# Two chunks of 256 tokens, q's tiles by halves, wider exponentials of the transposed q and reciprocal products on GpSimd, in a linear attention with a maxout feed-forward

## The chip, the core and the metric

The kernel runs on one core of one Trainium2 chip. TensorE (PE) multiplies into PSUM, eight banks of 128 x 512 floats. VectorE (DVE), ScalarE (ACT) and GpSimd (POOL) do the elementwise work; SyncE (SP) issues most DMAs. The metric is the device time of one execution, as a median of several runs, in microseconds (us).

## What is computed

Batch 8, 8 heads, 576 tokens, head size 64, 128 features; then a feed-forward of 512 to 768 to 512 on the 4608 tokens.

```python
def phi(x):
    proj = np.einsum('bhsd,df->bhsf', x, w_phi)
    proj = proj - np.max(np.abs(proj), axis=-1, keepdims=True)
    return np.concatenate([np.exp(proj), np.exp(-proj)], axis=-1)
q_p, k_p = (phi(q), phi(k))
kv = np.einsum('bhsf,bhsd->bhfd', k_p, v)
z = np.sum(k_p, axis=2)
num = np.einsum('bhsf,bhfd->bhsd', q_p, kv)
den = np.einsum('bhsf,bhf->bhs', q_p, z)[..., None] + 1e-06
x = (num / den), heads side by side: 4608 x 512
h = np.maximum(np.maximum(x @ w1, x @ w2), x @ w3)
out = h @ w_out
```

## The kernel before, in words

The attention is cut into 16 units, each four heads of one batch row. A unit has 18 tiles of 128 tokens for q and for k. 16 of q's tiles are the first 512 tokens of the four heads, the last two the ends (64 tokens a head). For each unit:

- q and k are loaded and cast to bf16 (units 0 to 3 by a casting DMA from GpSimd's queue; later units by a DMA from SP's queue and copies on GpSimd, L509, tile qk_bf). They are transposed into qkT, by TensorE for units 0 to 3 (tps, L494) and by a DMA later (L513).
- Projections psq and psk (L535), with tokens on the partitions. VectorE takes the row maxima mq and mk (L547). ScalarE writes the exponentials Ek of k, with both signs (L544), and em from mk (L557). GpSimd multiplies v by em into vab (L565). TensorE sums kvps (L586), copied to kv_sb (L592).
- Transposed projections psm of q, with features on the partitions (L606), in matmuls of 512 columns, one PSUM bank each. ScalarE takes the exponentials Eq of both signs from each bank (L612, eight instructions of 512 columns and two of 256 a unit).
- The tiles sq = exp(-2 mq) on ScalarE (L618, L619). The products psn of Eq and kv_sb (L637), for one head at a time: five tiles of 65 columns (64 values and the denominator) in one bank for each sign. VectorE scales the first bank by sq into y (L640, node kind "xu"), adds the second (L643, "xw"), takes the reciprocal of the denominators (L645, "xr"); the product with it goes to x_sb, on GpSimd or VectorE (L647, "x").
- x_sb is transposed into xT, by TensorE and a copy for units 0 to 5 (pxT, L657, L660), by a DMA on SP's queue later (L664).

The feed-forward subtracts w1 from w2 and w3 first (L762), so that the maximum is a ReLU and a max, and adds x @ (w1 @ w_out) again at the end. It works on nine chunks of 512 tokens: chunk b is the first 512 tokens of batch row b, chunk 8 the ends of all rows. A chunk is 12 up products of four 128 x 512 matmuls each (ups, L687). The first six are evacuated as a ReLU ("t1", on ScalarE L695 or VectorE L697), the other six as a maximum on VectorE ("h", L693), into hT. Then each of its four token tiles takes four matmuls from xT (L715) and six from hT (L720) into ops, a copy to osb (L728) and a store (L735).

The order of the work is written out in the string PLAN: each word names a node, the engine that does it, the buffer slots it takes, and after the @ the due time that a planner gave it. The kernel issues the nodes in the order of the words, so each engine has a fixed order and waits at its head. The due times and the costs in the nodes only sort the words; nothing waits for a clock. Before, a node of a unit for the product is one of these:

```python
n_ = nd("xu", {"DVE": 0.42}, lambda ...: nc.vector.tensor_tensor(...), ...)
n_ = nd("x", {"POOL": 1.42, "DVE": 0.74}, None, [n_], [y, rden, x_sb])
```

The keys are the engines allowed; PLAN says which one is taken.

Of the kernel before, what the change touches and what calls it, by code (L numbers as in the profile page):

```python
# [25 lines left out]
HU = 4  # L26
# [10 lines left out]
EARLY = 2  # L37
WARM = 28.0
# [46 lines left out]
8S0@0.7 5G0@1.2 6S@1.3 2S@1.9 0G@2.1 4G@2.6 10S0@3.1 92G1@3.5 9A@3.9 93G@4.3 11S0@4.4 177G2@5.2 7D@5.4 3D@5.9 176G@6.0  # L85
15T0@6.0 13T1@6.7 16D0@6.7 1173G@6.8 14D@7.4 34T000200@7.5 29T34@7.7 36A@8.0 38D@8.0 24T51@8.1 19T67@8.4 31A@8.4
94D@8.6 27D@8.7 20A@8.9 28D@9.3 26A@9.4 12G@9.8 32D@9.9 35A@9.9 96G@10.0 17T5@10.2 21A@10.4 178S0@10.4 18D@10.5
252G0@10.5 33D@10.8 30A@10.9 58T0500@10.9 23D@11.4 25A@11.4 253G@11.4 63T34@11.5 95S@11.7 60A@11.9 22D@12.0 39T16@12.1
1176G@12.2 401S0@12.3 62A@12.3 37D@12.6 44A0@12.8 59A@13.0 97T7@13.1 42D@13.2 47G0@13.2 45G@13.5 61A@13.5 43D@13.5
101T2@13.6 99T0@13.7 98D1@13.9 65A@14.0 100D@14.5 48A@14.5 108T117511@14.6 66A@14.7 46G@14.8 112D@15.1 41A@15.2  # L90
118T01@15.3 64A@15.5 102D@15.7 68T7@15.9 111D@15.9 67A@15.9 152T211@16.1 69A@16.4 122D@16.5 103T34@16.6 40A@16.7
256G@16.8 70A@17.0 51G@17.0 107D@17.1 110A@17.3 181G@17.3 113T60@17.3 49G@17.5 400S0@17.7 153A@17.7 106D@17.8
123T73@17.9 154A@18.2 117D@18.4 109A@18.5 184T2@18.6 50G@18.8 119A@18.9 116D@19.0 52T065@19.2 71A0@19.4 185D0@19.6
104A@19.6 115A@20.1 1174G@20.2 53D@20.2 182T2@20.3 126D@20.4 54A@20.6 121D@20.8 128A0@20.8 55T65@21.0 105A@21.0
127D@21.4 130G0@21.5 132A@21.5 183D@21.7 124A@21.7 75T47@21.8 57A@22.0 114A@22.2 56D@22.3 72T52@22.5 76D0@22.5
135A@22.7 134G@22.8 125A@22.8 186T6@22.9 73D@23.0 147T04@23.1 120A@23.1 187D@23.5 149A@23.6 80T35@23.6 77D@23.7
83T16@23.9 150A@24.1 133G@24.1 254D1@24.1 74D@24.2 1185T7@24.3 148A@24.6 81D1@24.6 1183T2@24.9 84D@25.0 151A@25.0
129G@25.4 82D@25.5 1187T3@25.5 1186A0@25.5 85D@25.9 142T51@26.2 78D0@26.3 139T040@26.4 131A@26.5 179D@26.5 1188D@26.6
1184A@26.6 79G0@26.7 180S@26.8 136T76@27.0 328S@27.4 146A@27.6 140D@27.8 259T2@27.9 86D1@28.0 327S@28.0 137A@28.1
138D@28.2 155A0@28.3 87G@28.4 261T4@28.4 141D@28.4 145A@28.5 159T36@28.6 329S@28.6 260D1@28.6 88T7@28.9 144A@29.0  # L100
262D@29.3 228T100@29.3 206T112011@29.4 160D0@29.5 143A@29.6 1175G@29.8 255S@29.9 210D@29.9 164T43@30.1 230A@30.1
161D@30.2 89A@30.4 156T52@30.4 165D1@30.7 90T6@30.8 157D@31.1 167T74@31.2 91A@31.4 166D@31.5 257T5@31.7 168D@31.9
207A@32.0 223T36@32.2 208A@32.4 169D@32.5 1193T7@32.6 225A@32.7 258D@32.9 224A@33.3 1D4@33.5 170D1@33.7 1189T5@33.9
158D@34.0 1194A@34.2 209D@34.4 227A@34.7 171D0@34.7 229A@35.2 197T7023@35.3 162D0@35.5 1190A@35.5 303T111@35.8
174T4@36.0 200D@36.0 304A@36.1 1191T5@36.3 226A@36.4 163D@36.6 202A@36.9 1177G@37.3 175D@37.4 305A@37.4 172T6@37.6
1192A@37.8 205D@37.9 1195T1@37.9 173A@38.3 204D@38.5 198A@39.0 201D@39.1 188T2654@39.3 1179G@39.4 203A@39.4
1201T7@39.8 199A@39.9 196D@40.0 1196A@40.4 192D@40.6 1199T0@40.7 193A@40.9 191D@41.2 1202A0@41.4 1178G@41.5
272T00152300@41.7 1200D@41.8 1209T7@42.2 278A@42.4 195D@42.4 189A@42.9 280D@43.0 1207T0@43.1 277A@43.4 407G2@43.6
276D@43.7 194A@43.8 1205T2@44.0 279D@44.3 1208A@44.3 403G@44.5 211A0@44.8 1203T4@44.8 1181D@44.9 190A@45.0 404G@45.1
1210D@45.5 274A@45.5 406G@45.7 281T63@45.8 218T01@45.9 1206A@46.0 284D@46.2 1217T7@46.2 1204A@46.5 285D@46.5  # L110
212G0@46.5 1180D@46.8 219A@47.0 1215T6@47.1 1182D@47.4 283A@47.5 221A@47.8 1211T4@48.0 1216D@48.2 282A@48.2 273A@48.5
1218D@48.8 1221T3@48.8 222A@49.0 213G@49.0 1212D@49.5 214A@49.5 220A@49.6 1213T2@49.7 275D@50.1 231A0@50.1 1219T4@50.6
1214D@50.8 1222D@51.5 405G@51.5 263T5176@51.5 331G0@51.8 408S0@51.9 215T002@52.0 1220D@52.1 264A@52.3 334G@52.3
267D@52.7 265A@52.9 333G@53.0 293T34@53.2 270D@53.3 217A@53.5 1223T5@53.5 332G@53.6 216A@53.8 266D@53.9 297A@54.1
240T20@54.4 271D@54.5 286A0@54.7 1224T@54.7 474S0@54.8 294A@54.9 287G0@55.0 241D0@55.1 296A@55.4 335S2@55.4 242D@55.7
295A@55.8 243T71@56.0 1225A0@56.3 232T02@56.4 298T34@56.8 268A@56.9 233D1@56.9 1231T5@57.1 244D@57.4 289A@57.4
288G@57.5 299A@57.6 245D@57.9 235T70@58.0 300A@58.2 1232T@58.3 544S@58.3 234D@58.3 269A@58.7 246D0@58.8 543S0@58.9
236D@59.0 302A@59.2 237D@59.6 475S@59.6 409T01612311@59.7 1233A1@59.9 247G0@60.0 238D1@60.1 290T007@60.2 413D@60.4
410A@60.5 473S@60.8 414A@60.9 417D@61.0 239G@61.4 306A0@61.4 1227T6@61.4 292D@61.6 291A@61.6 301A@62.0 416D@62.0
315T70@62.3 412D@62.6 310T24@62.6 415A@62.7 1228T@63.0 316D1@63.2 411A@63.3 311D0@63.6 317D@64.0 318T13@64.3 312D@64.4  # L120
1229A2@64.5 366T0200@64.7 549G0@64.8 319D@64.9 371T75@64.9 369A@65.2 307T46@65.3 479G2@65.4 320D@65.4 250T1@65.6
374A@65.7 308D@65.9 480G@66.0 1235T3@66.0 373A@66.1 321D1@66.3 251D@66.5 367A@66.6 322G1@66.7 1236T@66.9 309D@67.0
372A@67.1 313D0@67.6 370A@67.6 314D@67.9 550G@68.1 375A@68.1 325T7@68.2 248T2@68.5 368A@68.6 326D@68.8 323T6@68.8
614S0@68.9 249A@69.1 439T0111@69.3 478G@69.3 324D@69.4 427T75@69.5 684S@69.5 442A@69.7 354T104200@69.9 1237D3@69.9
547G@70.0 1241T6@70.1 330S1@70.1 441A@70.2 477G@70.5 431D@70.5 443A@70.7 357D@70.9 1247T3@70.9 440A@71.2 358D@71.2
1242D0@71.5 429A@71.7 336T4701@71.9 356A@71.9 430D@72.2 1248A@72.2 1249T6@72.5 344D@72.6 428A@72.7 620G1@72.8
355A@73.0 343D@73.2 1259T5@73.3 546G@73.5 1250A@73.6 340D@73.8 548G@74.1 341A@74.1 345T6023@74.3 619G@74.3 339D@74.4
613S0@74.5 342A@74.7 1243T4@74.8 349D@75.0 615S@75.1 346A@75.2 352D@75.7 338A@75.7 1245T1@75.7 1244A@76.2 348D@76.3
402S@76.3 1261T6@76.6 353D@76.9 1230S@76.9 359A0@77.0 337A@77.2 361G0@77.4 1255T4@77.5 1260D@77.5 481S1@77.5 362A@77.7
351A@77.9 1262D@78.1 1257T5@78.3 1246A@78.3 1256D@78.7 379A0@78.8 347A@79.0 418T2167@79.3 1258D@79.4 350A@79.5  # L130
# [161 lines left out]
def kernel(  # L292
# [562 lines left out]
```

## Time and profile before

| | before |
|---|---|
| median of 3 runs | 292.28 us (291.39 to 293.37) |
| the profiled execution's own time | 291.29 us |
| its span, first to last instruction | 289.5 us |
| PE busy | 268.4 us, 93% |
| DVE busy | 236.1 us, 82% |
| ACT busy | 199.7 us, 69% |
| POOL busy | 157.1 us, 54% |
| granted TensorE clock | 0.99 |

A group of the profile is a line: source line, engine, operation, tiles out<-in, shapes and count, then busy us and mean ns of one, then the idle time ahead of it and what ended it. Neighbours on an engine overlap, so a mean is longer than the distance from one start to the next. PE's busy time counts matmuls that wait in the pipeline, so a busy PE is not a PE at its peak. In the chain of work that ended last, PE has 76%, ACT 5%, DVE 4%, and the up products (L687) alone 30%.

### The profile page before, as it was taken

The page shows a single profiled execution, that of the slowest core. Times are in us where ns is not written, and L with a number is a line of the kernel's source. Part 1 is how long each engine was busy: PE and PEld are TensorE (multiplying, and loading weights), DVE is VectorE, ACT ScalarE, POOL GpSimd, SP SyncE. Part 2 cuts the span into 40 slices and gives each one's busy share as a digit, 9 for nine tenths or more (in the row PEclk, how much of TensorE's full clock was granted, in tenths as well). Part 3 has the DMA queues.
Part 4 walks back from the last instruction along what each step waited for, and adds up shares of the span by engine and source line. Part 5 has one row for each costly group of instructions (what it writes and reads, how often), then busy time and mean ns, then how long its engine had stood idle before and what let it go on. Part 6 is the DMA issues. An engine that isn't in the chain of part 4 may idle for free.

```text
span 289.5 us, 8537 instructions
## 1 busy us (share of the span) xinstructions
PE 268.4 (93%) x3461; PEld 151.7 (52%) x3502; DVE 236.1 (82%) x466; ACT 199.7 (69%) x486; POOL 157.1 (54%) x162
## 2 busy tenths in 40 slices
PE   1878899799999899999999999999999999999993
PEld 1557654356547555664565455655455564444442
DVE  1898889989997989999999988989999985246421
ACT  2797899598997698699855798999968470200020
POOL 8359478765757737672488593881935752000000
PEclk9997999999999999999999999999999999999998
DMA  8999992496699989957999898799045023020036
GB/s 156 227 247 255 253 271 87 77 207 209 210 258 223 262 238 340 240 138 163 334 211 175 221 267 202 233 102 224 20 121 151 5 48 84 0 109 2 36 148 143
DMA packets 70663, 49.93 MB, mean 172 GB/s; under 512 B 47072, under 2 KB 58720, under 8 KB 70624
## 3 DMA queue, kind: packets, MB, share of 16 engines
q1 hardware_dynamic: 65232, 44.25, 60.9%
q0 software_dynamic: 5312, 5.08, 10.8%
q8 instruction: 27, 0.44, 0.6%
q10 hardware_dynamic: 80, 0.07, 0.1%
q14 instruction: 12, 0.10, 0.1%
HBM read 34.67 MB, written 9.44 MB: 152 GB/s over the span
## 4 chain that ended last, share of the span: by engine, by line
PE 76%; ACT 5%; DVE 4%; issue 3%; DMA 2%; POOL 1%; SPq 0%; ACTq 0%; DVEq 0%
PE ups L687 30%; PE ops L720 13%; PE ops L715 9%; PE psn L637 7%; PE kvps L586 5%; PE psq L535 4%; ACT Eq L612 4%; PE psm L606 3%; PE pm L788 2%; DMA xT<-x_sb 2%; DVE hT L693 1%; PE psk L535 1%; ACT Ek L544 1%; DVE mk L547 1%; DMA out_dram<-osb 1%
## 5 line engine op out<-in xcount | busy, mean ns | idle before, releaser
L687 PE MATMUL ups<-xT,w_bf 128*128 128x512 bf16 x413 | 98.3, 379 | 2.7 <-DVE w_bf L762 1.5
L544 ACT ACTIVATE Ek<-psk 128x512 bf16<-128x512 f32 (+1 forms) x160 | 83.7, 581 | 15.9 <-PE psk L535 11.1
L565 POOL TENSOR_TENSOR vab<-v_raw,em 128x1152 bf16<-128x1152 f32 (+1 forms) x36 | 68.6, 1927 | 37.2 <-ACT em L557 33.4
L612 ACT ACTIVATE Eq<-psm 128x512 bf16<-128x512 f32 (+1 forms) x160 | 81.2, 585 | 7.8 <-PE psm L606 7.4
L687 PEld LDWEIGHTS <-w_bf 128*128 128x128 bf16 x432 | 39.8, 98 | 49.2 <-DVE w_bf L762 2.4
L720 PE MATMUL ops<-wout_bf,hT 128*128 128x512 bf16 (+1 forms) x217 | 50.7, 373 | 0.3 <-issue 0.2
L547 DVE TENSOR_REDUCE mq<-psq 128x4 f32<-128x512 f32 (+1 forms) x80 | 48.9, 627 | 1.4 <-PE psk L535 1.1
L547 DVE TENSOR_REDUCE mk<-psk 128x4 f32<-128x512 f32 (+1 forms) x80 | 48.2, 627 | 2.1 <-PE psk L535 0.9
L647 POOL TENSOR_TENSOR x_sb<-y,rden 128x640 bf16<-128x640 f32 x22 | 28.1, 1285 | 21.4 <-DVE rden L645 19.4
L693 DVE TENSOR_TENSOR hT<-hT,ups 128x512 bf16<-128x512 bf16 x54 | 35.8, 681 | 4.5 <-PE ups L687 3.9
L728 ACT COPY osb<-ops 128x512 f32<-128x512 f32 (+1 forms) x22 | 12.8, 581 | 37.6 <-PE ops L720 33.9
L640 DVE TENSOR_TENSOR y<-psn,sq 128x325 f32<-128x325 f32 x64 | 29.9, 489 | 4.2 <-PE psn L637 3.3
L637 PEld LDWEIGHTS <-Eq 128*128 128x128 bf16 x640 | 26.0, 99 | 11.9 <-issue 3.4
L720 PEld LDWEIGHTS <-hT 128*128 128x128 bf16 x222 | 20.4, 98 | 21.5 <-issue 0.3
L643 DVE TENSOR_TENSOR y<-y,psn 128x325 f32<-128x325 f32 x64 | 29.5, 484 | 1.3
L637 PE MATMUL psn<-kv_sb,Eq 128*128 128x65 bf16 x640 | 28.3, 196 | 1.7 <-DVE y L640 0.8
L695 ACT ACTIVATE hT<-ups 128x512 bf16<-128x512 f32 x31 | 18.3, 620 | 14.2 <-PE ups L687 13.9
L697 DVE TENSOR_SCALAR hT<-ups 128x512 bf16<-128x512 f32 x23 | 15.7, 686 | 14.1 <-PE ups L687 14.0
L535 PE MATMUL psq<-wph,qkT 64*128 64x128 bf16 x288 | 25.8, 225 | 0.7 <-ACT Ek L544 0.3
L535 PEld LDWEIGHTS <-qkT 64*128 64x128 bf16 x576 | 18.7, 97 | 14.7 <-issue 12.5
L535 PE MATMUL psk<-wph,qkT 64*128 64x128 bf16 x288 | 25.4, 225 | 0.3 <-DVE mq L547 0.2
L715 PE MATMUL ops<-xT 128*128 128x512 bf16 x82 | 23.8, 380 | 1.2 <-DVE mk L547 0.3
(59 smaller groups left out, 270.9 us busy)
## 6 DMA issues: line engine op xcount, KB each, us to landing
v_raw<-in_v_dram SPq DMA_DIRECT2D x16, 576.0 KB, 6.5
out_dram<-osb SPq DMA_DIRECT2D x32, 256.0 KB, 2.9
k_raw<-in_k_dram SPq DMA_DIRECT2D x12, 576.0 KB, 5.4
q_raw<-in_q_dram SPq DMA_DIRECT2D x12, 512.0 KB, 6.0
w_bf<-in_moe_w_dram POOLq DMA_DIRECT2D x3, 768.0 KB, 14.5
q_raw<-in_q_dram SPq DMA_DIRECT2D x16, 64.0 KB, 5.1
qk_bf<-in_k_dram POOLq DMA_DIRECT2D x3, 288.0 KB, 9.4
qk_bf<-in_q_dram POOLq DMA_DIRECT2D x3, 256.0 KB, 10.6
```

What stands on the lines that cost most here:

```text
L535: nc.tensor.matmul(ps()[:, i, :], lhsT=cols[r0:r0 + D, :], rhs=wph[r0:r0 + D, :], start=True, stop=True)
L544: "ek", {"ACT": 0.485 if n == 4 else 0.28}, lambda s=s, t0=t0, n=n, psk=psk: nc.scalar.activation(Ek[s]()[:, t0:t0 + n, :], psk()[:, 0:n, ...
L547: reds.append(nd(kind, {"DVE": 0.607 if n == 4 else 0.34}, lambda ps=ps, m=m, t0=t0, n=n: nc.vector.tensor_reduce(m()[:, t0:t0 + n], ps()[ ...
L565: made.append(any_of(n_, lambda n_, g=g, t0=t0, t1=t1: (nc.vector if n_.eng == "DVE" else nc.gpsimd).tensor_tensor(vab()[:, g, t0:t1, 0:D] ...
L612: "eq", {"ACT": 0.485 if n == 4 else 0.28}, lambda s=s, t0=t0, n=n, psm=psm: nc.scalar.activation(Eq[s]()[:, t0 * P:(t0 + n) * P], psm()[: ...
L637: nc.tensor.matmul(psn[g]()[:, c, :], lhsT=Eq[g]()[:, t0:t0 + P], rhs=kv()[:, pr, ab, g, :], start=True, stop=True)
L640: n_ = nd("xu", {"DVE": 0.42}, lambda pr=pr, ab=ab, psn=psn, y=y: nc.vector.tensor_tensor(y()[:, ab], psn[0](), sq()[:, 2 * pr + ab, :].un ...
L643: sums.append(nd("xw", {"DVE": 0.42}, lambda ab=ab, psn=psn, y=y: nc.vector.tensor_tensor(y()[:, ab], y()[:, ab], psn[1](), ALU.add), [n_] ...
L687: nc.tensor.matmul(ups(), lhsT=w_bf[i + 1][:, ct, j * P:(j + 1) * P], rhs=tokens_of(ct), start=(ct == 0), stop=(ct == CT - 1))
L693: nc.vector.tensor_tensor(hT()[:, j, :], hT()[:, j, :], ups(), ALU.max)
L715: nc.tensor.matmul(ops_()[:, 0:width], lhsT=tile_of(ct, tt), rhs=line_w[c_i > MOVE][:, ct, cols], start=(ct == 0), stop=False)
L720: nc.tensor.matmul(ops_()[:, 0:width], lhsT=hT()[:, j, tt * P:(tt + 1) * P], rhs=wout_bf[:, j, cols], start=False, stop=(j == JT - 1))
```

## The change

Five edits and a new PLAN, with the costs of many nodes set anew:

- Tiles of q are reordered: of each pair of heads, first the two tiles of tokens 0 to 255 of both, then those of 256 to 511 (tile_of_q; the casts on GpSimd become two of four tiles each). The products psn, y, the reciprocals and x go by halves (two tiles a head, then two and the end), two heads at a time.
- All eight banks are one tile (banks). psm takes two neighbouring banks, and one ScalarE instruction takes the exponential of 1024 columns.
- The scaling xu may go to ScalarE, which does it with one instruction of 65 columns for each tile and head, scaled by a column of sq. In the new PLAN 37 of 64 do.
- The product with the reciprocal is on GpSimd in all 64 cases. Units 14 and 15 are transposed by TensorE too (SOON; there reciprocals are taken for each pair of heads).
- Chunks 0 and 7 are done as two of 256 tokens, chunk 8 as 384 and 128; a chunk's first half waits for the first halves of its units only.

```diff
+SOON = (0, 1, 14, 15)
+SPLIT = (0, 7)
...
+    def tile_of_q(t):
+        pr, half, ab, c = t // 8, t // 4 % 2, t // 2 % 2, t % 2
+        return 8 * pr + 4 * ab + 2 * half + c if t < MT else t
...
+                    for half in range(2):
+                        copy_on[n_.eng](
+                            qk()[:, t0 + 4 * half:t0 + 4 * half + 4, col:col + D].rearrange("p (a j) d -> p a j d", a=2),
+                            raw_part(u, c, t0, t0 + 8).rearrange("p (a h j) d -> p a h j d", a=2, h=2)[:, :, half])
...
-                        "eq", {"ACT": 0.485 if n == 4 else 0.28}, lambda s=s, t0=t0, n=n, psm=psm: nc.scalar.activation(
-                            Eq[s]()[:, t0 * P:(t0 + n) * P], psm()[:, 0:n * P], EXP, scale=1.0 - 2.0 * s), [a], [psm, Eq[s]], locks=[psm]))
+                psm = Buf(slots.setdefault("bank", Slots(8)), lambda b: banks[:, b.index:b.index + 2, :], 2)
...
+                n_ = nd("eq", {"ACT": 0.905 if len(parts) == 2 else 0.265}, lambda s=s, psm=psm, to=to: nc.scalar.activation(
+                    to(), psm(), EXP, scale=1.0 - 2.0 * s), [a], [psm, Eq[s]], locks=[psm])
...
-                n_ = nd("xu", {"DVE": 0.42}, lambda pr=pr, ab=ab, psn=psn, y=y: nc.vector.tensor_tensor(
-                    y()[:, ab], psn[0](), sq()[:, 2 * pr + ab, :].unsqueeze(2).to_broadcast([P, 5, W]), ALU.mult),
+                n_ = nd("xu", {"DVE": 0.07 + 0.14 * nt, "ACT": 0.2 * nt}, None, [a, n_sq], [psn[0], sq, y], locks=[psn[0]])
...
+                    for ab in range(2):
+                        for c in range(nt):
+                            nc.scalar.mul(y()[:, pr, ab, c, :], psn[0]()[:, ab, c, :], sq()[:, pr, half, ab, c:c + 1])
...
-            n_ = nd("x", {"POOL": 1.42, "DVE": 0.74}, None, [n_], [y, rden, x_sb])
+                    m = nd("x", {"POOL": 0.155 + 0.209 * nt}, None, [n_], [y, rden, x_sb])
...
-        if u < X_PE:
+            if u < X_PE or u in SOON:
...
+        for c0, n in ([(0, 256), (256, 256)] if b in SPLIT else [(0, SM)]):
...
+    for b0, b1 in ((0, 6), (6, 8)):
+        chunk(B, lasts[b0:b1], b0 * ST, (b1 - b0) * ST, lambda ct, b0=b0, b1=b1: xT[:, b0:b1, ct, SM:SM + ST],
```

In PLAN's new order the four weight loads stand together on GpSimd's queue ahead of unit 0's vab; the first 384 tokens of chunk 8 stand between units 12 and 14; four subtractions of the weights are on GpSimd and two on VectorE (before three and three).

More of the change, by code (lines that the diff above doesn't have):

```diff
@@ L90 @@
[L90 to L94, printed above, removed]
@@ L273, in fill @@
             if b.pool is pool and b is not spare:
-                x = spans.setdefault(id(b), [b.index, n.start, n.end])
-                x[1], x[2] = min(x[1], n.start), max(x[2], n.end)
+                for i in range(b.width):
+                    x = spans.setdefault((id(b), i), [b.index + i, n.start, n.end])
+                    x[1], x[2] = min(x[1], n.start), max(x[2], n.end)
     for n in order:
@@ L336, in fixed, with make @@
         return Buf(pool, lambda b: tiles[b.index])
+    banks = psum.tile([P, 8, SM], FP32, name="banks")
     def bank(name, shape, dtype=FP32):
-        pool = slots.setdefault("bank", Slots(8))
-        return Buf(pool, lambda b: psum.tile(shape, dtype, name=name, tag=f"b{b.index}"))
+        per = 1
+        for n in shape[1:]:
+            per *= n
+        names = "abcd"[:len(shape) - 1]
+        sizes = {c: n for c, n in zip(names, shape[1:])}
+        def make(b):
+            x = banks[:, b.index, :]
+            x = (x if dtype == FP32 else x.bitcast(dtype))[:, 0:per]
+            return x.rearrange(f"p ({' '.join(names)}) -> p {' '.join(names)}", **sizes) if len(names) > 1 else x
+        return Buf(slots.setdefault("bank", Slots(8)), make)
     nodes = []
@@ L650, in attention @@
[L650 to L662 removed]
+        divs, done = [], []
@@ L663, in xdma @@
+        if not done:
             def xdma():
@@ L728, in ev @@
                     copy_on[n_.eng](part()[:, 0:width], ops_()[:, 0:width])
-                e = ff("osb", {"ACT": 0.61, "DVE": 0.62} if halves == 1 else {("ACT", "DVE")[i]: 0.35}, None, [a], [ops_, part],
+                e = ff("osb", {"ACT": 0.53, "DVE": 0.61} if halves == 1 else {("ACT", "DVE")[i]: 0.35}, None, [a], [ops_, part],
                        locks=[ops_])
@@ L798 @@
         rows = out[b * S:b * S + SM, :].rearrange("(p j) n -> p j n", j=SM // P)
-        chunk(b, units[2 * b]["done"] + units[2 * b + 1]["done"], lambda ct, b=b: xT[:, b, ct, 0:SM],
-              lambda ct, tt, b=b: xT[:, b, ct, tt * P:(tt + 1) * P],
-              lambda tt, rows=rows: [(rows[:, tt, :], slice(0, P))], 1)
+        hT = buf("hT", 2, [P, JT, SM], BF16)
+        for c0, n in ([(0, 256), (256, 256)] if b in SPLIT else [(0, SM)]):
+            ready = [x for u in (2 * b, 2 * b + 1) for half in range(2) if 256 * half < c0 + n and c0 < 256 * half + 256
+                     for x in units[u]["done"][half]]
+            chunk(b, ready, c0, n, lambda ct, b=b, c0=c0, n=n: xT[:, b, ct, c0:c0 + n],
+                  lambda ct, tt, b=b: xT[:, b, ct, tt * P:(tt + 1) * P],
+                  lambda tt, rows=rows: [(rows[:, tt, :], slice(0, P))], 1, hT)
         if b == MOVE:
-            for n in units[UNITS - 2]["done"] + units[UNITS - 1]["done"]:
-                n.deps += straights[0] + lines[1]
+            for u in (UNITS - 2, UNITS - 1):
+                for n in units[u]["done"][0] + units[u]["done"][1]:
+                    n.deps += straights[0] + lines[1]
     lasts = []
@@ L821, in fn @@
         def fn():
-            idler = psum.tile([P, SM], FP32, name="idler", tag=f"b{i}")
-            nc.tensor.matmul(idler, lhsT=idle, rhs=idle.unsqueeze(1).to_broadcast([P, 4, P]), start=True, stop=True)
+            nc.tensor.matmul(banks[:, i, :], lhsT=idle, rhs=idle.unsqueeze(1).to_broadcast([P, 4, P]), start=True, stop=True)
         return fn
```

497 lines of the change are left out of this document (269 added, 228 removed).

## The prediction

> **What bounds the kernel now.** I read the busy time of each engine first, cut into stages, then the waits, then the groups by shape, then single lines of the timeline. The stages are cut at the first up product (tile ups, L687) of chunks 0 to 7. The columns of the windows are the engines' busy time with the count of instructions, the granted clock, the DMA share and GB/s.
>
> ```profile
> core 0: us, PE busy (x) PEld busy (x) DVE busy (x) ACT busy (x) POOL busy (x), PEclk, DMA share, GB/s
> 0.00:43.10 43.10, 32.29 (x557) 22.69 (x558) 32.84 (x73) 32.71 (x80) 27.82 (x37) 0.96 1.11 234
> 43.10:74.80 31.70, 29.73 (x401) 16.51 (x404) 30.01 (x55) 26.34 (x63) 23.75 (x23) 1.00 0.57 136
> 74.80:105.80 31.00, 30.08 (x414) 16.95 (x420) 27.74 (x57) 26.19 (x66) 19.90 (x21) 1.00 0.99 249
> 105.80:135.40 29.60, 29.04 (x406) 16.14 (x413) 28.77 (x58) 25.24 (x66) 16.87 (x16) 1.00 0.87 229
> 135.40:163.20 27.80, 27.04 (x396) 15.47 (x401) 26.66 (x54) 19.28 (x48) 19.70 (x20) 1.00 1.01 224
> 163.20:196.30 33.10, 32.16 (x508) 18.55 (x512) 30.18 (x63) 31.19 (x78) 22.87 (x21) 1.00 0.91 211
> 196.30:223.50 27.20, 26.99 (x372) 14.73 (x372) 25.75 (x50) 23.55 (x56) 14.76 (x13) 1.00 0.52 122
> 223.50:246.70 23.20, 22.88 (x244) 12.47 (x245) 18.15 (x38) 9.69 (x25) 11.46 (x14) 1.00 0.23 57
> 246.70:289.50 42.80, 38.20 (x184) 18.22 (x186) 15.96 (x25) 5.48 (x10) 0.00 (x0) 0.97 0.24 74
> ```
>
> To be seen: in six stages from 43 to 223 us VectorE is busy 89 to 97% of the time beside a TensorE that is rarely idle, ScalarE 69 to 94%, GpSimd 54 to 75%. From 247 us on TensorE works alone. So an edit pays if it takes work off VectorE, as long as nothing else fills in its place.
>
> ```profile
> POOL x_sb L647 <- DVE rden L645: 19.4, 9, 4.8
> POOL qk_bf L486 <- DMA q_raw<-in_q_dram: 6.1, 2, 3.6
> 249.31 11.82 PE ups L687 x54
> 70.11 4.03 ACT Eq L612 x8
> ```
>
> The first two lines are waits (total, times, longest), the others pieces of the chain (start, us, what). GpSimd waits for rows of VectorE and, once, 3.6 us for the ends of q at the start. TensorE alone does a 512-column matmul in 11.82/54 = 0.219 us, and ScalarE an exponential of 512 columns in 4.03/8 = 0.50.
>
> ```profile
> L544 ACT ACTIVATE Ek<-psk 128x512 bf16<-128x512 f32 x128 | 73.3, 623 | 13.2 <-PE psk L535 10.7 <-DVE mk L547 2.4
> L544 ACT ACTIVATE Ek<-psk 128x256 bf16<-128x256 f32 x32 | 12.6, 412 | 2.7 <-DVE mk L547 2.3 <-PE psk L535 0.4
> L565 POOL TENSOR_TENSOR vab<-v_raw,em 128x1152 bf16<-128x1152 f32 x28 | 59.5, 2146 | 37.2 <-ACT em L557 33.4 <-PE psn L637 3.0 <-DMA v_raw<-in_v_dram 0.8
> L565 POOL TENSOR_TENSOR vab<-v_raw,em 128x576 bf16<-128x576 f32 x8 | 9.0, 1160 | 0.0
> L647 POOL TENSOR_TENSOR x_sb<-y,rden 128x640 bf16<-128x640 f32 x22 | 28.1, 1285 | 21.4 <-DVE rden L645 19.4 <-PE psn L637 1.2 <-DVE v_raw L478 0.6
> L647 DVE TENSOR_TENSOR x_sb<-y,rden 128x640 bf16<-128x640 f32 x10 | 10.5, 1051 | 0.2
> L640 DVE TENSOR_TENSOR y<-psn,sq 128x325 f32<-128x325 f32 x64 | 29.9, 489 | 4.2 <-PE psn L637 3.3 <-ACT kv_sb L592 0.7
> L619 ACT ACTIVATE sq<-mq 128x4 f32<-128x4 f32 x16 | 3.7, 234 | 0.0
> 20.44 0.29 ACT L618 ACTIVATE sq<-mq 128x16 f32<-128x16 f32 x1
> 20.55 0.27 ACT L619 ACTIVATE sq<-mq 128x4 f32<-128x4 f32 x1
> ```
>
> The groups give busy us and mean ns of one; the last two lines are single instructions (start, us). Two neighbours on ScalarE overlap: 20.44 and 20.55 start 0.11 apart though each takes over 0.27.
>
> **The change, part by part.** Counts are from the order of the built program.
>
> Exponentials of q: 128 of 512 columns become 64 of 1024. By the two Ek rows a column costs (623-412)/256 = 0.82 ns, so 1024 start 0.48+0.42 = 0.90 apart: 0.06 saved a pair, 64 times 3.8 us off ScalarE. Between no saving and that I take it whole, since 256 and 512 columns fit one line.
>
> Scaling of y (xu): VectorE did 64. It keeps 27, and 37 go to ScalarE, which can only do 65 columns at a time there: 182 copies, each scaled by a value read from the tile sq. VectorE loses 37 x 0.40 (0.489 less the overlap) = 15 us. No ScalarE row of before takes its scale from a tile. The price of one lies between 0.11 (the two sq lines' distance) and 0.26 (the 234 ns of the sq row with no overlap, and 0.03 for more columns): 20 to 47 us. I take 0.234, the whole duration of the sq row, because it is the nearest small f32 row that writes SBUF and nothing shows that fetching a scale is hidden: 42.6 us. The Trainium skill ("ScalarE: Activation LUTs", section "What ACT_TABLE_LOAD costs") gives 186 ns and 0.833 a column with an immediate scale, 93 more for each pointer operand, and 93 of overlap between neighbours. By it the copies would start 0.24 apart (an estimate), 44 us in all, where the same figures without the pointer give 0.15 and 27 us; the trace agrees with the overlap (0.11 apart for 0.2 of duration), and no run shows the pointer.
>
> The sum xw on VectorE now waits for the last of four or six ScalarE copies. Behind it on VectorE stand the row maxima of the next unit (mq, mk), which hold the PSUM banks that TensorE's next projections need, so a late copy is paid by all three.
>
> Products with the reciprocal (x): 10 on VectorE (0.75 apart) and 22 on GpSimd become 64 on GpSimd. VectorE loses 7.5. GpSimd costs (2146-1160)/576 = 1.71 ns an element and 0.17 fixed: 0.61 for 256 elements, 0.83 for 384, 32 x 1.44 = 46 us against 28.1.
>
> Casts of q on GpSimd: 24 instructions become 54, since the tiles are reordered by halves; at 0.26 fixed each (678 ns for 512 columns, 367 for 128, group L509) 7.8 us more. One subtraction of the weights moves from VectorE (1.49) to GpSimd (2.34).
>
> Chunks 0, 7 and the last one in two pieces: 144 more matmuls, shorter, so the columns stay; 36 more evacuations at up to 0.16 fixed (group L728 on VectorE: 686 ns for 512 columns, 424 for 256), at most 6 us over two engines. Units 14 and 15 are transposed on TensorE (20 x 0.062 = 1.2 us, four copies of 0.4) and not by DMA; those two leave SP's queue, where nothing waited for them (TensorE had ops work up to 246.7).
>
> Order: 384 of the last chunk's 512 tokens are placed ahead of the last units: 12 x 4 x 0.16 + 3 x 2.16 = 14 us of TensorE work leaves the end. The four weight loads stand together on GpSimd's queue, ahead of unit 0's vab and of unit 3's loads; DMA is full there anyway (1.11), so bytes only change places: within 2 us either way. The ends of q are taken after vab, so the 3.6 us wait no longer holds vab.
>
> **The sum.** I add what stands on each engine between the same first products, at the start-to-start times above (GpSimd's sum comes out 3% over its busy time in before and is cut by that). The fullest engine, and what the stage lasted beyond it:
>
> ```
> stage        1     2     3     4     5     6     7     8
> before  PE 28.2  28.5  27.5  26.6  30.3  26.0  23.2  38.0
>        DVE 29.4  25.5  27.9  25.9  28.6  24.1  17.3  14.7
>        gap  2.3   2.5   1.7   1.2   2.8   1.2   0.0   4.8
> after   PE 28.7  29.0  27.7  28.7  25.7  40.1  25.8  24.0
>        DVE 27.8  27.4  26.3  23.1  22.0  27.0  18.8  13.0
>        ACT 28.5  30.9  29.8  26.4  18.7  28.8  16.2   2.9
>       POOL 31.4  28.6  27.0  23.2  15.3  14.9  10.8   0.0
> ```
>
> With the gap of its own stage, and 1.2 in stage 5 where only PE is left full: 33.7, 33.4, 31.5, 29.9, 26.9, 41.3, 25.8, 28.8. Stage 0: ScalarE gains 4.3 (34.1 for 29.8) and loses nothing it waited for; GpSimd's 3.6 wait goes; I leave it at 43.1. Together 294.4, that is 4.9 over the span of 289.5. The profiled execution took 291.29; the median of the three runs is 292.28, so 297.2, which I call 297: slower by 1.6%.
>
> **Rivals.**
> A, the copies are cheap. At 0.11 ScalarE has 25.5, 27.7, 26.1 in stages 1 to 3, below PE or POOL; stages 2 and 3 become 31.5 and 29.4, stage 0 some 41: 288.3, which is 1.2 under the span, time 291. For it: neighbours overlap in every row. It decides below 0.16 a copy, where stage 2's ScalarE (24.9 without its 26 copies) meets TensorE's 29.0.
> B, faster: TensorE always has work ready. The place is the gap: with VectorE relieved by 7 us and the last chunk's 14 us as filling, stages 1 to 4 keep only the 1.2 that stages 4 and 6 show where PE leads, and stage 0 gains the whole 3.6. With A's price, and stage 1 at POOL's 31.4: 39.5+32.6+30.2+28.9+29.9+26.9+41.3+25.8+28.8 = 283.9, time 286.7. It needs A's price and holds up to 0.15 a copy. Against it: stages 2 and 3 have POOL within 1 us of PE, so two engines are full.
> C, GpSimd is the bound. If its small pieces cost 0.2 us more than the line through the vab rows (the 64 products and 30 more casts), stages 1 to 3 gain 2 to 3 us each: 303. For it: the queue stands at 31.4 in a stage of 31.7. Against it: the 640-element row (1285) is on the line.
>
> **How the numbers follow.** Forecast 0.48 (time 294 to 301), A 0.24, B 0.16, C 0.12. A run of this kernel tells about 1% (3 us) from no change. Slower by over 1% (above 295.2): 0.45 of the forecast and C, 0.57. Within 1%: 0.03, 0.22 of A and 0.02 of B, 0.27. Faster: 0.14 of B and 0.02 of A, 0.16. The forecast's own range is 294 to 301; the range given, 287.5 to 303, leaves out half of B and half of C.
>
> **What would show it.** Right: the copies of y on ScalarE start over 0.2 apart; ScalarE busy over 92% of stages 2 and 3; more time of VectorE waiting for y from ScalarE; GpSimd over 90% in stage 1; stage 8 at 28 to 29. Wrong: copies 0.11 to 0.15 apart, or ScalarE under 85% there; or TensorE's gap under 1.2 in stages 1 to 4; or products on GpSimd far from 0.61 and 0.83.

## The result, and the profile after

The changed kernel takes 303.78 us (302.76 to 304.45), the kernel before 292.82 (291.39 to 293.60) beside it on the same chip: ratio 1.040, 95% interval 1.037 to 1.044. It is slower by 4%; the forecast was 1.6%, and 303.78 lies just outside its range. Some executions of one kernel come out some 2% slower than its others; the medians here count all of them, the ratios leave those slower ones out. The profiled execution has a span of 302.4 us, 12.9 over that of before.

The windows of the changed kernel, cut like those of before at the first up product of chunks 0 to 7 (now L752; columns as before):

```profile
core 0: us, PE busy (x) PEld busy (x) DVE busy (x) ACT busy (x) POOL busy (x), PEclk, DMA share, GB/s
0.00:47.95 47.95, 33.38 (x557) 23.72 (x558) 33.88 (x72) 36.04 (x92) 30.64 (x43) 0.86 0.94 186
47.95:80.03 32.08, 31.33 (x473) 21.92 (x470) 28.41 (x65) 29.55 (x87) 28.98 (x41) 1.00 0.83 244
80.03:113.27 33.24, 31.74 (x446) 17.73 (x445) 29.07 (x57) 31.20 (x85) 27.00 (x39) 1.00 1.01 231
113.27:145.51 32.24, 30.01 (x506) 17.51 (x502) 27.61 (x60) 30.76 (x84) 26.21 (x42) 1.00 0.92 223
145.51:176.26 30.75, 30.27 (x383) 15.94 (x380) 24.18 (x45) 26.49 (x63) 21.24 (x30) 1.00 0.89 234
176.26:204.34 28.08, 26.90 (x377) 14.74 (x375) 23.48 (x46) 21.38 (x63) 14.94 (x15) 1.00 0.65 171
204.34:247.32 42.98, 41.55 (x391) 21.84 (x388) 29.49 (x57) 30.10 (x77) 15.60 (x17) 1.00 0.27 58
247.32:273.73 26.41, 26.07 (x350) 14.86 (x348) 20.32 (x43) 16.80 (x44) 9.84 (x10) 1.00 0.13 49
273.73:302.41 28.68, 24.58 (x210) 18.17 (x208) 14.54 (x36) 2.78 (x8) 0.79 (x2) 0.96 0.19 65
```

To be seen: ScalarE (ACT), not VectorE, is now the fullest elementwise engine, 92 to 95% of stages 1 to 3. Against the forecast the stages miss by +4.9, -1.6, -0.2, +0.7, +0.9, +1.2, +1.7, +0.6 and -0.1 us. Stage 0 alone is 4.9 of the 8.0, and its granted clock fell from 0.96 to 0.86. In stages 1 to 7 the granted clock is 1.00 before and after.

The groups that the forecast priced, and the heads of two views of the changed kernel, the chain that ended last (shares by engine) and one wait (total, times, longest):

```profile
L655 ACT ACTIVATE Eq<-banks 128x1024 bf16<-128x1024 f32 x64 | 65.6, 1060 | 5.1 <-PE banks L646 4.9
L697 ACT ACTIVATE y<-banks,sq 128x65 f32<-128x65 f32 x182 | 40.2, 341 | 7.3 <-POOL x_sb L711 4.2 <-PE banks L684 2.8 <-ACT Ek L579 0.2
L711 POOL TENSOR_TENSOR x_sb<-y,rden 128x384 bf16<-128x384 f32 x32 | 26.1, 826 | 23.2 <-DVE rden L705 21.1 <-ACT y L697 2.1
L711 POOL TENSOR_TENSOR x_sb<-y,rden 128x256 bf16<-128x256 f32 x32 | 19.3, 615 | 9.9 <-DVE rden L705 6.3 <-ACT sq L665 3.6
```
```profile
PE 59%; ACT 17%; POOL 9%; DMA 6%; issue 4%; DVE 3%; SPq 1%; ACTq 0%; POOLq 0%; DVEq 0%
```
```profile
DVE y L699 <- ACT y L697: 11.0, 18, 2.1
```

ScalarE's share of the chain rose from 5 to 17%, TensorE's fell from 76 to 59%, and VectorE waits 11 us in all for the scaled copies, a wait that before did not have. In runs of copies without a pause the starts are 0.197 us apart (median of 158).

The chain through stage 0 of the changed kernel (start, us, what):

```profile
3.60 5.54 DMA q_raw<-in_q_dram
...
11.19 0.31 POOL qk_bf L510
...
11.51 9.39 DMA q_raw<-in_q_dram
...
22.66 0.28 POOL qk_bf L510
```

It runs through the ends of q: those of units 0 and 1 must land and be cast (the last cast is at 11.19) before the one q_raw buffer can take those of units 2 and 3. Those land at 20.9 and 22.6 us, are cast (22.66), and TensorE transposes them at 22.98. In the new order this small batch stands on TensorE's queue ahead of unit 0's products psn; before, it stood behind the first of them.

### The profile page after: what moved, and what is told of

Same layout as the page of the kernel before. It is cut to its first block, busy times and chain, and to the rows that moved or that the text cites. A ratio compares the mean times of both kernels' runs of the same rounds, so it can differ in the third digit from the quotient of the medians.

```text
span 302.4 us, 9177 instructions
## 1 busy us (share of the span) xinstructions
PE 275.8 (91%) x3666; PEld 166.4 (55%) x3666; DVE 231.0 (76%) x475; ACT 225.1 (74%) x596; POOL 175.2 (58%) x234
## 4 chain that ended last, share of the span: by engine, by line
PE 59%; ACT 17%; POOL 9%; DMA 6%; issue 4%; DVE 3%; SPq 1%; ACTq 0%; POOLq 0%; DVEq 0%
PE banks L752 24%; PE banks L785 11%; ACT y L697 9%; PE banks L780 8%; DMA q_raw<-in_q_dram 5%; PE banks L621 5%; PE banks L570 4%; POOL vab L600 4%; ACT Eq L655 3%; PE banks L684 3%; POOL x_sb L711 3%; ACT Ek L579 2%; PE banks L646 2%; DMA qkT<-qk_bf 2%; PE banks L853 1%
## 5 line engine op out<-in xcount | busy, mean ns | idle before, releaser
L752 PE MATMUL banks<-xT,w_bf 128*128 128x512 bf16 (+3 forms) x576 | 100.5, 326 | 0.3 <-DVE hT L758 0.2
L579 ACT ACTIVATE Ek<-banks 128x512 bf16<-128x512 f32 (+1 forms) x160 | 84.8, 583 | 12.5 <-PE banks L570 8.9
L655 ACT ACTIVATE Eq<-banks 128x1024 bf16<-128x1024 f32 (+1 forms) x96 | 77.1, 848 | 6.5 <-PE banks L646 6.3
L752 PEld LDWEIGHTS <-w_bf 128*128 128x128 bf16 x576 | 52.2, 98 | 38.7 <-issue 3.3
L711 POOL TENSOR_TENSOR x_sb<-y,rden 128x384 bf16<-128x384 f32 (+1 forms) x64 | 44.7, 721 | 33.1 <-DVE rden L705 27.4
L582 DVE TENSOR_REDUCE mq<-banks 128x4 f32<-128x512 f32 (+1 forms) x80 | 48.8, 627 | 4.9 <-PE banks L570 4.3
L785 PE MATMUL banks<-wout_bf,hT 128*128 128x512 bf16 (+1 forms) x222 | 52.3, 374 | 0.0
L582 DVE TENSOR_REDUCE mk<-banks 128x4 f32<-128x512 f32 (+1 forms) x80 | 49.1, 627 | 2.5 <-PE banks L570 1.1
L697 ACT ACTIVATE y<-banks,sq 128x65 f32<-128x65 f32 x182 | 40.2, 341 | 7.3 <-POOL x_sb L711 4.2
L758 DVE TENSOR_TENSOR hT<-hT,banks 128x512 bf16<-128x512 bf16 (+3 forms) x72 | 38.5, 549 | 6.7 <-PE banks L752 4.5
L699 DVE TENSOR_TENSOR y<-y,banks 128x260 f32<-128x260 f32 (+1 forms) x64 | 30.3, 489 | 12.8 <-ACT y L697 11.0
L684 PEld LDWEIGHTS <-Eq 128*128 128x128 bf16 x640 | 25.2, 99 | 9.2 <-issue 3.5
L684 PE MATMUL banks<-kv_sb,Eq 128*128 128x65 bf16 x640 | 27.6, 196 | 1.7 <-ACT y L697 1.4
```

The source lines that it names most:

```text
L579: "ek", {"ACT": 0.485 if n == 4 else 0.28}, lambda s=s, t0=t0, n=n, psk=psk: nc.scalar.activation(Ek[s]()[:, t0:t0 + n, :], psk()[:, 0:n, ...
L582: reds.append(nd(kind, {"DVE": 0.607 if n == 4 else 0.34}, lambda ps=ps, m=m, t0=t0, n=n: nc.vector.tensor_reduce(m()[:, t0:t0 + n], ps()[ ...
L655: n_ = nd("eq", {"ACT": 0.905 if len(parts) == 2 else 0.265}, lambda s=s, psm=psm, to=to: nc.scalar.activation(to(), psm(), EXP, scale=1.0 ...
L684: nc.tensor.matmul(psn[g]()[:, ab, c, :], lhsT=Eq[g]()[:, t0:t0 + P], rhs=kv()[:, pr, ab, g, :], start=True, stop=True)
L697: nc.scalar.mul(y()[:, pr, ab, c, :], psn[0]()[:, ab, c, :], sq()[:, pr, half, ab, c:c + 1])
L711: nc.vector if n_.eng == "DVE" else nc.gpsimd).tensor_tensor(
```

## The experiments

Each is an edit of the changed kernel (labels e) or of the kernel before (b). Ratios are to the kernel before on the same chip, with 95% intervals; the changed kernel's is 1.040. The line numbers of most edited kernels lie up to 50 lower than in the changed kernel (L650 is L697 there). Stages are cut as above.

**The price of the copies.** Two edits of L697:

```diff
-nc.scalar.mul(y()[:, pr, ab, c, :], psn[0]()[:, ab, c, :], sq()[:, pr, half, ab, c:c + 1])
+nc.scalar.mul(y()[:, pr, ab, c, :], psn[0]()[:, ab, c, :], 1.0)                 # e1_imm
+nc.scalar.mul(y()[:, pr, :, 0:nt, :], psn[0]()[:, :, 0:nt, :], 1.0)             # e2_one, one for all tiles
```

> Edit: the changed kernel, its 182 copies of 65 columns on ScalarE scaled by the constant 1 and not by a column of sq (leaves out the scaling). Theory P (fetching the scale is part of the price of a copy, and ScalarE is the fullest engine of stages 1 to 4): copies start 0.15 us apart, not 0.20, ScalarE loses 182 x 0.05 = 9 us, the time falls 2 to 4 us, to 300 to 302. Rival N (the fetch is hidden, 0.20 is what any such small instruction costs): 0.20 apart still, time within 1 us of 303.8.

> Edit: the changed kernel, but each xu on ScalarE is one instruction over all its 260 or 390 columns, scaled by the constant 1 (leaves out the scaling by sq): 37 instructions for 182. At the slope of the exponentials, 0.82 ns a column and some 0.1 fixed, they start 0.3 to 0.42 apart, ScalarE loses 36 - 13 = 23 us. Theory S (ScalarE's copies hold stages 1 to 4 and part of stage 0): time falls 5 to 8 us, to 296 to 299. Rival O (TensorE, GpSimd and the order of the work hold these stages, ScalarE is only filled beside them): falls under 2 us.

e1_imm: 293.16 us, ratio 1.002 (0.998 to 1.007). e2_one: 292.76, 1.004 (1.001 to 1.008). The group of e1_imm:

```profile
L650 ACT ACTIVATE y<-banks 128x65 f32<-128x65 f32 x182 | 24.5, 260 | 9.3 <-POOL x_sb L664 4.9 <-PE banks L637 4.1
```

With a constant as the scale the copies start 0.104 us apart, not 0.197: the fetch costs 0.093 each, 182 x 0.093 = 17 us of ScalarE. Theory P is right, its sizes were too small: the median falls 10.6 us and the span of the profiled execution 12.2, in every stage with copies (stages 0 to 7: 3.5, 1.6, 0.9, 1.4, 1.0, 1.4, 1.9, 0.5), also in stages 4 to 7, where ScalarE is 64 to 86% busy. In stages 1 to 7, 8.7 us together, the granted clock is 1.00 in both; the 3.5 of stage 0 come with another clock, as the next experiment shows. Fewer, longer instructions (e2_one) take another 9 us off ScalarE's busy sum (24.5 to 15.6 in the group) and bring nothing more: theory S has the direction right, but nearly all of the gain is the fetch's.

**The small batch ahead of unit 0's products.** In PLAN:

```diff
-186T2@18.7   -187D@19.1
+186T6@25.85  +187D@26.1
```

> Edit: the changed kernel with one batch moved on TensorE's queue: the two transposes of unit 2's ends of q (tiles 16 and 17) and their copy stand behind unit 0's products psn, not ahead of them. Nothing else moves. Theory Q (stage 0 grew from 43.1 to 48.0 us because TensorE stands 3 to 4 us at this batch, which waits for the ends of q behind the weight loads, and unit 0's products, and then VectorE, ScalarE and GpSimd, wait with it): the products of unit 0 start at 21.8 us for 23.5, where kv_sb comes free, and stage 0 falls by 1 to 2.5 us, the time with it, to 301.3 to 302.8. Rival F (ScalarE and VectorE have a stage of full work there, the wait is made up by chunk 0): within 0.7 us of 303.8.

302.07 us, ratio 1.035 (1.031 to 1.039); stage 0 is 45.74, by 2.2 shorter. TensorE's timeline of the changed kernel and then of e3_tail (L637 is L684, the products psn):

```profile
22.98 0.30 PE L518 MATMUL banks<-ident,qk_bf 128*64 128x128 bf16 x4 [1.50 <-POOL qk_bf L510]
23.54 0.43 PE L684 MATMUL banks<-kv_sb,Eq 128*128 128x65 bf16 x8
```
```profile
20.84 0.43 PE L637 MATMUL banks<-kv_sb,Eq 128*128 128x65 bf16 x8
```

The products start at 20.84 for 23.54. Theory Q is right that the batch costs 2 us. It is wrong that this is how stage 0 grew: in the trace of before the first products start at 24.2, later than in the changed kernel. From the first products to chunk 0's first up product there are 18.9 us before (43.12 - 24.22), 24.4 in the changed kernel, 24.9 in e3_tail and 20.5 in e1_imm. So the growth lies behind them; the batch wastes a lead of some 3 us that the new order had.

The fetches are not the only thing that differs there. The granted clock was 0.50 for 10.2 us behind the products in the changed kernel, and for 3.4 us in e1_imm, as before (24.41 to 27.82). The windows of these stretches, the changed kernel and then e1_imm:

```profile
23.92:34.16 10.24, 8.73 (x92) 6.12 (x91) 8.45 (x20) 9.47 (x31) 5.36 (x8) 0.50 1.18 211
24.05:27.47 3.42, 3.33 (x43) 2.78 (x44) 3.05 (x9) 2.91 (x14) 1.08 (x2) 0.50 1.21 220
```

Two later runs with cheap copies (e17_late, e18_early) had no such stretch behind the products, and there the rest of stage 0 took 19.7 us. One run has cheap copies and 10.2 us at 0.50 (e9_imm_tail, with the batch moved): 23.1 us, for 24.9 in e3_tail, which has the same order, the fetches, and 10.2 us at 0.50 too. That pair leaves 1.8 us for the 22 fetches of stage 0 (22 x 0.093 = 2.0); it is one execution of each, and that of e9_imm_tail took 294.48 us for a median of 291.54. How the growth of stage 0 divides between the fetches and the clock, and whether the one brings on the other, is not shown.

**The weight loads ahead of unit 0's vab.**

```diff
-1158G@10.6 1157G@11.4 1156G@12.2
+1158G@17.42 1157G@17.44 1156G@17.46
```

> Edit: the changed kernel with three of the four weight loads issued on GpSimd's queue behind unit 0's four products vab, not ahead of them; the first stays. The products vab start 2.3 us sooner, and the ends of q share the DMA engines with one weight load and not four. Theory D (the wait at the small batch comes from the weight loads ahead of it): the ends of q land at 18 to 20 us, not 22.6, the batch is done by 20.5, stage 0 falls by 1.5 to 3 us, the time to 301 to 302.3. Rival L (the weights are then late, the subtractions wait for them): no change or up to 3 us more.

305.23 us, 1.044 (1.039 to 1.048). Theory D's landing at 18 to 20 us did not come: the ends of q still took 10.3 us to land (issued 13.37, landed 23.66; before the edit 12.16 and 22.58), and the time fits rival L's "no change". The test is not a clean one, since the three weight loads moved were issued from 17.85 to 20.2 us, before the ends had landed. The batch began at 24.06 and stage 0 took 49.58. Over the five executions with the batch in place and the scales fetched, stage 0 follows this landing: 22.6, 22.7, 22.8, 23.7 and 24.0 us gave 47.95, 48.13, 48.37, 49.58 and 49.98.

**ScalarE's queue or VectorE's wait?** e4_512 splits each 1024-column exponential again; e12_nowait writes the copies to a tile of their own, and the sum takes sq in their place.

> Edit: the changed kernel with each exponential of 1024 columns of the transposed q as two of 512 again (128 for 64). If the wide form saves 0.06 us a pair, ScalarE gains 3.8 us. Theory S (ScalarE holds stages 1 to 4): time up by 1 to 3 us, 305 to 307. Rival O (ScalarE does not hold them): within 0.7 us. If the wide form saves nothing, ScalarE's busy sum shows it.

> Edit: the changed kernel with its 182 copies on ScalarE as they are, scaled by columns of sq and in the same places of its queue, but written to a tile of their own; the sums xw behind them on VectorE take sq in place of the scaled product, so VectorE does not wait for ScalarE (leaves the scaled product out of 37 sums). Theory W (the 10 to 12 us that the fetch costs come in by way of VectorE, which waits for the copies 11 us in all): 293 to 296, near the run with the cheap copies. Rival K (they come in by way of ScalarE's own queue: the exponentials behind the copies are late, and the banks): 300 to 304.

```diff
-    y()[:, pr, :, 0:nt, :], y()[:, pr, :, 0:nt, :], psn[1]()[:, :, 0:nt, :], ALU.add)
+    y()[:, pr, :, 0:nt, :], y()[:, pr, :, 0:nt, :] if n_.eng == "DVE" else
+    sq()[:, pr, half, :, 0:nt].unsqueeze(3).to_broadcast([P, 2, nt, W]), psn[1]()[:, :, 0:nt, :], ALU.add)
```

e4_512: 304.76 us, 1.044 (1.040 to 1.048); the exponentials start 0.477 apart for 0.903 a pair, 64 x 0.05 = 3.3 us more on ScalarE, and the change in time is within the intervals. That lies between theory S and rival O and decides neither. e12_nowait: 300.91 us, 1.032 (1.025 to 1.040). With VectorE's wait gone, stages 1 to 7 are 1.8 us shorter together (the profiled execution took 304.64, the other three 300.2 to 301.0). So most of the price does not come in by VectorE's wait; theory W falls and rival K's time is right. TensorE itself still waits 7.6 us in all for the copies in this trace.

**As much work elsewhere on ScalarE.** The cheap copies, and 64 useless ones, 0.294 us apart, 18.8 us in all: behind the 1024-column exponentials (e14_aside), spread over the last 100 us (e17_late), over stages 1 to 4 (e18_early).

```diff
+nc.scalar.copy(aside, ident.unsqueeze(1).to_broadcast([P, 2, P]))
```

> Edit: the changed kernel with copies scaled by the constant 1 (293.2 us; leaves out the scaling by sq), and 64 useless copies of 256 bf16 columns, read from SBUF, directly behind ScalarE's exponentials of 1024 columns: 64 x 0.26 = 17 us more on ScalarE, as much as the fetches of sq cost, but not between a product and its sum. Theory W (what counts is that VectorE waits for the copy): 293 to 298. Rival T (what counts is ScalarE's total): 301 to 305.

> Edit: the changed kernel with copies scaled by the constant 1 (293.2 us; leaves out the scaling by sq) and 64 useless ScalarE copies of 256 bf16 columns, 0.29 us apart each, 19 us in all, directly behind exponentials and evacuations of the last 100 us, where ScalarE is busy 65% in the trace without them. Theory B (ScalarE's work is paid in the stretches where its queue is full, and nearly free elsewhere): 293 to 296. Rival U (it is paid everywhere alike, some 43% as in the run with the same copies spread over the kernel): 300 to 303.

> Edit: as the run before, but the 64 useless copies stand behind exponentials and evacuations of stages 1 to 4, where ScalarE is busy near 90% without them. Theory B: paid at 70 to 100%, 306 to 312. Rival U (43%, as spread over the kernel): 300 to 303.

301.34 us, 1.030 (1.025 to 1.035); 300.66, 1.034 (1.027 to 1.041); 302.10, 1.033 (1.024 to 1.041). Rival T is right, then rival U: over a long stretch the same work costs about half its time wherever it stands. By the stages, against e1_imm: e14_aside 7.9 us in stages 1 to 7, where 55 of the 64 copies stand (49% of 16.2), e17_late 9.3 in stages 6 and 7 with 61 of them (52% of 17.9), e18_early 9.9 in stages 1 to 4 with all (53% of 18.8). The fetches outside stage 0 are 160 x 0.093 = 14.9 us and cost 8.7 there (58%). A single stage can be far from that: e14_aside paid 22% in stage 6 and 78% in stage 1. Stage 6 of e1_imm, then of e17_late:

```profile
194.53:235.61 41.08, 41.08 (x392) 21.74 (x388) 29.11 (x57) 27.48 (x77) 15.45 (x17) 1.00 0.29 63
```
```profile
192.57:239.30 46.73, 42.20 (x386) 22.08 (x388) 30.23 (x58) 38.03 (x114) 15.49 (x17) 1.00 0.28 63
```

ScalarE has 13.6 of 41.1 us free in the first and TensorE is always busy; 10.6 us more on ScalarE make the stage 5.7 longer, and TensorE's idle time goes from none to 4.5. All the waits of TensorE that the profile lists in this stage of e17_late, 4.0 us, end with ScalarE; in e1_imm it lists none. The longest three:

```profile
PE banks L600 <- ACT Eq L609: 1.5, 2, 0.8
PE banks L706 <- ACT Ek L533: 0.9, 1, 0.9
PE banks L524 <- ACT Eq L609: 0.7, 1, 0.7
```

So TensorE waits for ScalarE, for its exponentials (Eq, Ek) above all. And the free time of ScalarE is one of the stage's average: in e17_late it is busy 22.5 of the 22.6 us from 198.4 to 221.0 and 4.6 of the 12.3 behind them.

**The scalings on VectorE again, or the exchange.** In PLAN the engine letters of nodes: all 37 xu from A to D (e5_dve); that and the batch moved (e6_dve_tail); of these 37 only the 20 whose sum VectorE had waited for by over 0.1 us (e15_mix); all 37, and 28 evacuations t1 from D to A (e16_swap). The last three have the batch moved, and all four compute the whole.

> Edit: the changed kernel with all 37 scalings xu back on VectorE (one instruction each, scaled by sq as it should be), the order of the work as it is. ScalarE loses 36 us, VectorE gains 37 x 0.40 = 15 us. Theory S (the 182 copies at 0.20 us hold the work, and VectorE has room since products and part of the tail left it): 292 to 296, some 8 to 11 under the changed kernel. Rival V (VectorE takes over as the bound, 246 us busy): 298 to 304.

> Edit: the changed kernel with all scalings xu on VectorE and the small batch of unit 2's ends of q behind unit 0's products on TensorE's queue, both edits together. If the two costs add (theory: two separate places): 1.5 to 2.5 us below the run with the first edit alone, so 290 to 294. If not (one covers the other in stage 0): within 0.7 us of it.

> Edit: the changed kernel with the small batch of unit 2's ends of q behind unit 0's products, and with 20 of the 37 scalings xu of ScalarE on VectorE: those whose sum VectorE waited for by over 0.1 us in the trace of the changed kernel. The computation is whole. Theory W: the waits go (11 us) and VectorE gains 20 x 0.40 = 8 us where it was waiting: 292 to 296, at or under the run with all scalings on VectorE (295.9). Rival: the waits move to the 17 that stay, 297 to 301.

> Edit: the changed kernel with the small batch behind unit 0's products, all 37 scalings xu on VectorE, and in exchange 28 evacuations t1 (a ReLU, no scale to fetch) from VectorE to ScalarE: VectorE 15 us more and some 15 less, ScalarE 36 less and some 12 more. The computation is whole. Theory (work that needs no scale from a tile is what ScalarE can take, and VectorE's total is what makes all scalings on VectorE 295.9): 289 to 293, at or under the kernel before. Rival (the time hangs on waits for order, not on VectorE's total): 294 to 297.

299.91 us, 1.027 (1.023 to 1.032); 295.88, 1.015 (1.010 to 1.019); 294.99, 1.011 (1.007 to 1.014); 300.20, 1.028 (1.023 to 1.033). Rival V is right for the first: VectorE takes part of the price over. The batch costs there as well, 4.0 us between the medians and 2.1 in stage 0 of the profiled executions: the two costs add. e15_mix comes out where theory W put it, and VectorE no longer waits for the copies; but ScalarE has 104 fetching copies fewer too, so the run does not tell the wait from the work. The exchange refutes its theory and lies above its rival as well: 15 us off VectorE (busy 240.5 to 225.7) bring nothing and 12 more on ScalarE (188.3 to 200.1) cost 4.3 us over e6_dve_tail. e15_mix is the fastest whole version of the changed kernel, not clear of e6_dve_tail, and still 1% slower than before.

**Parts of the change alone, and both costs out.** b7_pool: the ten products x of VectorE on GpSimd in PLAN. b8_act: 37 xu of the kernel before on ScalarE, five copies each; b9_imm: the same scaled by 1.0. e9_imm_tail: e1_imm and e3_tail together. e11_cast: q's casts in one piece.

```diff
+for c in range(5):
+    nc.scalar.mul(y()[:, ab, c, :], psn[0]()[:, c, :], sq()[:, 2 * pr + ab, c:c + 1])
```

> Edit: the kernel before with its ten products x of VectorE put on GpSimd, in place in the order; this is one part of the change alone. VectorE loses 7.5 us, GpSimd gains 13 us. Theory S (the products are not what made the change slow): within 2 us of before, 289 to 293. Rival C (GpSimd's queue comes to hold the work): 3 to 6 us slower than before.

> Edit: the changed kernel with q's casts on GpSimd again in one piece of 512 columns (30 instructions fewer; leaves out the order of tokens by halves). GpSimd loses up to 7.8 us. Theory S (GpSimd is not what holds the stages): within 1.5 us of the changed kernel, 302.3 to 304. Rival C (GpSimd's queue holds stages 1 to 3): 2 to 4 us less.

> Edit: the kernel before with 37 of its 64 scalings xu on ScalarE, as many in each unit as in the changed kernel, five copies of 65 columns each scaled by a column of sq (185 copies), in place in the order; this is one part of the change alone. VectorE loses 15 us, ScalarE gains 185 x 0.20 = 36 us. Theory S (a copy that fetches its scale is paid for by the time at some 60%, wherever it stands): 7 to 14 us slower than before, 298 to 305. Rival O (it is the new order that cannot stand them; VectorE was the fullest before and is relieved): within 3 us of before, or faster.

> Edit: the kernel before with 37 scalings on ScalarE in 185 copies, scaled by the constant 1 (leaves out the scaling by sq). ScalarE has 17 us less than with the scale fetched from sq (320.7 us), 19 us more than in the kernel before, VectorE 15 less than there. Theory P (the fetch alone is what is expensive, each us of it paid in full): 302 to 305. Rival Q (any copies in ScalarE's queue delay the sums on VectorE and so the banks, whatever they cost): 308 to 318. Third: back to 290 to 295, ScalarE simply had no room for more than 19 us.

> Edit: the changed kernel with copies on ScalarE scaled by the constant 1 (leaves out the scaling by sq) and with the small batch of unit 2's ends of q behind unit 0's products; both costs found so far taken out. Theory S (these two are what the change loses, and its other parts bring a little): 0.5 to 1% under the kernel before, 288 to 290, stage 0 at 42 to 43. Rival R (the other parts lose as well: products and casts on GpSimd, more pieces): within 0.5% of before or over it, above 290.5.

b7_pool: 293.19 us, 1.006 (1.003 to 1.008). e11_cast: 304.02, 1.041 (1.037 to 1.045). Both are as theory S had it: GpSimd's added work is not what made the change slow. b8_act: 320.71, 1.099 (1.094 to 1.103), over twice what I expected. b9_imm: 302.88, 1.037 (1.033 to 1.041), theory P. In the old order the fetch, 185 x 0.093 = 17.2 us, costs 17.8, all of it, and the bare copies cost 11 us though they relieve VectorE of 15. The waits of VectorE for them in b8_act, then in b9_imm:

```profile
DVE y L649 <- ACT y L647: 36.4, 29, 3.5
```
```profile
DVE y L649 <- ACT y L647: 21.5, 24, 2.6
```

e9_imm_tail: 291.54 us, 0.998 (0.995 to 1.001). With both costs out the change is worth nothing either way; rival R is nearer than the gain of 0.5 to 1% that I hoped for.

## Why the prediction was wrong, step by step

- "I leave it at 43.1" is the step that failed. Stage 0 took 47.95: 4.9 of the 8.0 us that the span was over the sum. ScalarE's 4.3 us more (3.3 measured, 36.04 for 32.71 busy) were taken as hidden. Behind unit 0's first products the stage lasts 24.4 us, 20.5 with cheap copies, 18.9 before. The forecast had no term for the clock either, which was 0.50 for 10.2 us there and for 3.4 in the other two; how much of the growth is the fetch and how much the clock stays open.
- "The fullest engine, and what the stage lasted beyond it" was the wrong way to price work on ScalarE, and a second error hid it. In stages 4 to 7 the fullest engine of the sum is TensorE, so ScalarE's copies stand there at nothing; the fetches alone cost 4.8 us there (1.0, 1.4, 1.9 and 0.5 in e1_imm), and these stages came out 4.4 over the sum. At the measured 0.197 the forecast's own two cases (294.4 at 0.234, 288.3 at 0.11: 49 us for each us of price) give 292.6, 9.8 under the span. They make the fetch worth 0.093 x 49 = 4.6 us; it cost 12.2 of the span, 8.7 of them where the clock was 1.00. In the new order ScalarE's work is paid at 49 to 58% over the stretches tried, also where it is 60 to 67% busy on average; in the old order the fetch was paid in full.
- The price of a copy: 0.197, inside the bounds, 0.234 taken. The Trainium skill ("ScalarE: Activation LUTs", section "What ACT_TABLE_LOAD costs") gives 93 ns for a pointer operand; the trace agrees (0.197 - 0.104). By its overlap of 93 ns the copies would start 0.24 apart, an estimate; here neighbours overlap by some 0.14 (median duration 0.334 with the pointer, 0.248 without).
- "The sum xw on VectorE now waits": it does, 11 us, but that is the smaller way in (1.8 us of stages 1 to 7 by e12_nowait).
- "The ends of q are taken after vab, so the 3.6 us wait no longer holds vab": true on GpSimd. The same ends were then late for TensorE, whose queue I had not read for them; that costs 2 us.
- The weight loads "only change places": e10_wlater, which moved three of them, came out 1.5 us higher with overlapping intervals, so nothing speaks against it.
- Exponentials (0.90 forecast, 0.903), products on GpSimd (0.61 and 0.83; 0.615 and 0.826) and stage 8 (28.8; 28.68) were right. Stage 1 came out 1.6 shorter than GpSimd's queue with a gap made it, and rival C is refuted by b7_pool and e11_cast.
- Four signs of "Right" came (ScalarE 94 and 95% busy in stages 2 and 3, VectorE's waits, GpSimd 90% in stage 1, stage 8), and the copies missed 0.2 by 0.003, while the time left the range: the signs tested the prices, none of them the way in which they were added up.
- The cuts of before at 74.80 and 135.40 lie 0.2 and 0.4 us off the first up products (74.97 and 134.99); that shifts time between neighbouring stages and leaves the sum as it is.
- Rival A's size was right but for 2 us (291; 293.16 at 0.104). Rival B's gain is not there even with both costs out.

By which wait TensorE pays can be read in part. In the changed kernel it waits 7.4 us in all for ScalarE, 5.8 of them for the scaled copies, which hold the banks that its next matmuls write; in e1_imm 0.9, none of them for copies. The longest, of the changed kernel:

```profile
PE banks L570 <- ACT y L697: 2.4, 4, 1.3
PE banks L684 <- ACT y L697: 1.4, 2, 0.8
PE banks L780 <- ACT y L697: 1.1, 2, 0.7
```

What stays open: these waits are inferred by the profile and no edit takes them away alone; their difference is 6.5 us for a cost of 12.2, and where the rest comes in is not shown. Nor is it shown why the fetch is paid in full in the old order and at about half in the new one, and how stage 0's growth divides between the fetches and the clock.

## What to carry to other kernels

Work that is put on an engine whose results TensorE waits for at every step is not free because the engine has idle time on average: cut its busy time finer than a stage, look for waits of TensorE that end with it, and price the work at half or more until a run says otherwise (here 49 to 58%, in another order 100%). Read the granted clock beside every stage before its growth is put down to one cause. Before splitting one broadcast operation into many small ones, price one with its scale read from a tile, since the fetch can cost nearly as much as the copy (0.093 and 0.104 us here). When a transfer's wait is taken off one queue, look for every other queue on which its result stands ahead of something needed.

## What was not expected of the hardware

- A ScalarE instruction of 65 f32 columns that reads its scale from a tile starts the next one 0.197 us later, with a constant 0.104: the fetch lengthens the distance by its whole 0.093.
- Splitting cheap copies costs nothing in time: 182 of 65 columns or 37 of 260 and 390 gave 293.16 and 292.76 us.
- The second of the two small loads of q's ends of units 2 and 3 (64 KB) took 9.6 to 10.4 us to land in the traces of before, of the changed kernel and of e10_wlater, however the four weight loads stood around it.
